# Attention in two resolutions and an ELU feed-forward: the order of all steps behind batch 0 written out as one list

## The chip, the cores and the metric

The kernel runs on one core of a Trainium2 chip. The metric is the device time of the program in microseconds. A core has five instruction queues that run beside each other, each in its own order: PE (TensorE, matrix products), DVE (VectorE), ACT (ScalarE), POOL (GpSimd) and SP (SyncE, which here only issues DMAs). ACT and POOL can issue DMAs too. Matrix products go to PSUM, which has few banks, so a bank must be read out before PE can write it again.

## What is computed

Eight batches of eight heads, 576 positions of 64 numbers. Each head has a local attention (only keys less than 4 positions away) and an attention over sequences shortened by the mean of each four positions; the two results are added. The sum, as 4608 tokens of 512 numbers, goes through two dense layers with an ELU between them.

```python
q_d = q.reshape(B, H, Sd, factor, D).mean(axis=3)        # same for k and v; factor = 4
out_up = np.repeat(sm_attn(q_d, k_d, v_d), factor, axis=2)
mask = np.abs(pos[:, None] - pos[None, :]) < factor
scores = np.where(mask, scale * np.matmul(q, k.transpose(0, 1, 3, 2)), -1000000000.0)
attn_out = out_up + softmax(scores) @ v
x = np.ascontiguousarray(attn_out.transpose(0, 2, 1, 3)).reshape(B * S, H * D)
h = x @ w_in                                             # 512 -> 2048
g = np.where(h > 0.0, h, alpha * (np.exp(np.minimum(h, 0.0)) - 1.0))
out = g @ w_out                                          # 2048 -> 512
```

## The kernel before

Attention works on pairs of heads, four pairs j to a batch b. For a pair the steps are: load q, k and v (SP, L165 and L178) into one of 11 fp32 stage buffers; cast them to fp16 on POOL (L201, L204, L211), which frees the stage; turn q and k on PE by products with an identity (L223, L232), which also sums fours; copy the turned tiles to SBUF (ACT, with sums on DVE); sum v in fours on PE (L285); scores (L311, L321); exp on ACT (L333, L339); mask on DVE (L348). After the four pairs come the denominators (PE L374) and their reciprocal (DVE L380). The reciprocals are spread over partitions: in batches 0 and 1 by matmuls with SEL (L410), later through DRAM, with a store of rd (L385) and a load of rcb (L395) on ACT's queue. Then the output products (L438, L444), two multiplications on DVE (L455, L458) and one or two additions on POOL (L465) that write x.

The dense layers work on nine tiles t of 512 tokens. mm1 has 16 steps of four 512-column matmuls (L498); behind each stand an exp on ACT (L503), a min-and-add (L504) and a max-and-add (L507) on DVE. mm2 has 16 steps of four matmuls (L518); each fourth ends a block of 128 tokens, which ACT copies to os (L524) and SP stores (L526). A batch is 576 tokens and a tile 512, so tile t needs parts of one or two batches: tile 0 only batch 0, tile 1 the last 64 tokens of batch 0 and 448 of batch 1.

Nothing moves an instruction after it is recorded (`manual_schedule`, L529): each engine runs its instructions in the order in which the Python code makes them. Batch 0 is made by `first_batch`. After it, functions that each record the steps of several engines (`mm1`, `mm2`, `scores`, `transposes`, `outputs`, `second_loads` and others) are given a time by `at(time, fn, ...)`, and the events are recorded sorted by that time. A function's steps thus enter all queues together: `mm2` records matmuls, copy and store in one go, `mm1` matmuls, exp and both elu steps.

The weights are loaded by `wload` on POOL's queue (L146): four parts of WI in batch 0, between the third and the fourth cast of v, and four parts of WO at the end of batch 0. Batch 1's first load waits through a 1x1 copy on POOL (L158) that reads element `gts[0][0:1, 7, 0:1]`, so it starts when the eighth elu of tile 0 is done.

Of the kernel before, what the change touches and what calls it, by code (L numbers as in the profile page):

```python
# [71 lines left out]
def kernel(  # L72
# [188 lines left out]
    def copy_k(b, j, tk, copy, copy_sums):  # L261
        _, kt, kd = stT[(b, j)]
        t4 = tk[:, :, 0:GW].rearrange("p g (c w) -> p g c w", w=QW)
        copy(
            out=kt[:, PAD : PAD + S].rearrange("p (g c u) -> p g c u", g=2, c=3),
            in_=t4[:, :, :, 0:QB],
        )
        copy_sums(
            out=kd[:].rearrange("p (g c n) -> p g c n", g=2, c=3), in_=t4[:, :, :, QB:QW]
        )  # L270

# [23 lines left out]

    def transposes(b, j):
        tq, tk = two("tq"), two("tk")
        new_qk(b, j)
        turned(b, j, "q", tq)
        vsum_mm(b, j, tq[:, :, GW : GW + 128])  # L300
        turned(b, j, "k", tk)
        copy_q(b, j, tq, nc.scalar.copy)
        vsum_copy(b, j, tq[:, :, GW : GW + 128])
        copy_k(b, j, tk, nc.scalar.copy, nc.vector.tensor_copy)
# [45 lines left out]
    def scores(b, j):  # L350
        sc = [two("sc"), two("sc")]
        sc_local(b, j, sc)
        sc_down(b, j, sc)
        for e in range(2):
            exp_local(b, j, sc, e)
            exp_down(b, j, sc, e)
        masked(b, j)
        stT.pop((b, j))


    def denominators(b, den):
# [118 lines left out]
    def outputs(b, j0):  # L480
        rcb = stR[b]
        lgs = {}
        for j in (j0, j0 + 1):
            lgs[j] = two("lg")
            out_mm(b, j, lgs[j])
        for j in (j0, j0 + 1):
            out_x(b, j, lgs[j], rcb)
# [4 lines left out]
    def mm1(t, fc):
        if fc == 0:
            gts[t] = sb.tile([128, FCN, TBLK], FP16, tag="gt", bufs=2, name="gt")
        hp = bank("misc" if t == 0 and fc % 2 else "hp", "hp")
        x = xts[t]
        for dc in range(DMC):
            nc.tensor.matmul(  # L498
                hp[:], WI[:, dc, 128 * fc : 128 * fc + 128], x[:, dc, :],
                start=(dc == 0), stop=(dc == DMC - 1),  # L500
            )
        e = sb.tile([128, TBLK], FP16, tag="e", bufs=3, name="e")
        nc.scalar.activation(out=e[:], in_=hp[:], func=AF.Exp)  # L503
        nc.vector.tensor_scalar(  # L504
            out=e[:], in0=e[:], scalar1=1.0, scalar2=-1.0, op0=AB.min, op1=AB.add
        )
        nc.vector.scalar_tensor_tensor(  # L507
            out=gts[t][:, fc, :], in0=hp[:], scalar=0.0, op0=AB.max, in1=e[:], op1=AB.add
        )

    def mm2(t, i):

        tt, part = i // 4, i % 4
        if part == 0:
            ops[t] = bank("misc", "op")
        op_ = ops[t]
        for fc in range(4 * part, 4 * part + 4):
            nc.tensor.matmul(  # L518
                op_[:], gts[t][:, fc, 128 * tt : 128 * tt + 128], WO[:, fc, :],
                start=(fc == 0), stop=(fc == FCN - 1),  # L520
            )
# [218 lines left out]
```

## Time and profile before

| | us |
|---|---|
| median of 3 runs | 403.9 |
| lowest and highest run | 394.77 and 430.42 |
| the profiled execution | 396.93 |
| its span, first to last instruction | 395.1 |

| engine | busy us | share of the span |
|---|---|---|
| PE, matmuls | 355.3 | 90% |
| DVE | 244.8 | 62% |
| ACT | 204.2 | 52% |
| POOL | 127.1 | 32% |

The page cuts the span into 40 slices of some 9.9 us; a digit is the busy share of a slice in tenths, and PEclk is the clock granted to PE:

```profile
PE   2778988948876898899999999999999999999996
DVE  2845964433875665796579748966885675555510
POOL 2548062065541582183218322831240040000000
PEclk9999999686997899999999999999999999999999
DMA  8989993069999997977784958543000500100112
```

A share over the whole span is a mean of stages with different limits, so a stage is read from its own slices. A busy PE is not always PE at its full pace: the pace follows from how many matmuls a stretch holds. A row of the timeline has the start, the duration, the engine, the line and the operation, and in brackets how long the engine stood idle before and what ended that.

### The profile page before, as it was taken

The numbers are of one execution on the slowest core, as the hardware profiler recorded it, in microseconds if no ns is written. First come the engines' busy times: TensorE is split into PE (matmuls) and PEld (weight loads), VectorE is DVE, ScalarE is ACT, GpSimd is POOL, SyncE is SP. The second block draws the span as 40 slices with busy tenths as digits, with TensorE's granted clock in tenths as the row PEclk, the third lists the DMA queues.
The fourth block names the chain that finished last, engine by engine and source line by source line (L and its number), as shares of the span: only waits on it lengthen the run. The fifth ranks groups of instructions, "written<-read, shape, count | busy, mean of one in ns | idle before, by whom it ended". The sixth has DMA issues, their size and how long they took to land.

```text
span 395.1 us, 9269 instructions
## 1 busy us (share of the span) xinstructions
PE 355.3 (90%) x3792; PEld 189.8 (48%) x3792; DVE 244.8 (62%) x468; ACT 204.2 (52%) x389; POOL 127.1 (32%) x181
## 2 busy tenths in 40 slices
PE   2778988948876898899999999999999999999996
PEld 2664444624443455455545555555554444444442
DVE  2845964433875665796579748966885675555510
ACT  3533657234865375657566655667474434444321
POOL 2548062065541582183218322831240040000000
PEclk9999999686997899999999999999999999999999
DMA  8989993069999997977784958543000500100112
GB/s 262 170 131 144 238 276 105 2 126 200 200 183 154 163 201 136 190 151 153 138 192 94 181 127 177 115 96 103 29 28 30 128 28 28 53 27 36 46 53 80
DMA packets 116260, 49.17 MB, mean 124 GB/s; under 512 B 102154, under 2 KB 109434, under 8 KB 116218
## 3 DMA queue, kind: packets, MB, share of 16 engines
q1 hardware_dynamic: 107082, 39.33, 49.5%
q0 software_dynamic: 4224, 4.19, 6.7%
q10 hardware_dynamic: 4912, 5.07, 5.9%
q8 instruction: 29, 0.48, 0.6%
q14 instruction: 13, 0.11, 0.1%
HBM read 43.23 MB, written 9.55 MB: 134 GB/s over the span
## 4 chain that ended last, share of the span: by engine, by line
PE 70%; DMA 14%; ACT 5%; DVE 5%; POOL 2%; issue 2%; ACTq 1%; SPq 0%; POOLq 0%; DVEq 0%
PE op L518 30%; PE hp L498 26%; DMA v<-in_v_dram 4%; DMA rd<-rc 4%; PE lg L438 2%; PE sc L311 2%; ACT pex L333 2%; DMA rcb<-rd 2%; PE tq L285 2%; DVE gt L507 2%; PE den L374 2%; DMA SEL<-SELc 2%; PE tq L223 2%; PE tk L223 1%; DMA q<-in_q_dram 1%
## 5 line engine op out<-in xcount | busy, mean ns | idle before, releaser
L498 PE MATMUL hp<-xt,WI 128*128 128x512 f16 x576 | 150.9, 390 | 2.8 <-DVE gt L507 1.7
L518 PE MATMUL op<-WO,gt 128*128 128x512 f16 x576 | 145.7, 382 | 0.0
L503 ACT ACTIVATE e<-hp 128x512 f16<-128x512 f32 x144 | 86.5, 602 | 102.1 <-PE hp L498 88.9
L507 DVE SCALAR_TENSOR_TENSOR gt<-hp,e 128x512 f16<-128x512 f32 x144 | 99.6, 692 | 5.4
L504 DVE TENSOR_SCALAR e<-e 128x512 f16<-128x512 f16 x144 | 55.4, 384 | 56.8 <-ACT e L503 54.6
L498 PEld LDWEIGHTS <-WI 128*128 128x128 f16 x576 | 54.9, 100 | 67.1 <-issue 10.4
L518 PEld LDWEIGHTS <-gt 128*128 128x128 f16 x576 | 54.2, 98 | 64.1 <-issue 1.3
L465 POOL TENSOR_TENSOR xt<-ln,gn 128x64 f16<-128x64 f16 (+7 forms) x64 | 42.1, 688 | 122.2 <-DVE ln L458 122.2
L333 ACT ACTIVATE pex<-sc 112x576 f16<-112x576 f32 x64 | 41.0, 647 | 14.5 <-PE sc L321 10.3
L348 DVE TENSOR_TENSOR mex<-pex,MASK 112x1152 f16<-112x1152 f16 x32 | 27.0, 843 | 25.6 <-ACT pex L333 25.3
L259 ACT CAST qt<-tq 128x720 f16<-128x720 f32 x24 | 18.3, 763 | 29.9 <-PE tq L285 27.6
L211 POOL CAST v<-v 112x768 f16<-112x768 f32 x32 | 28.7, 898 | 12.1 <-DMA v<-in_v_dram 12.1
L204 POOL CAST q<-q 96x768 f16<-96x768 f32 x24 | 20.8, 868 | 33.2 <-issue 21.2
L524 ACT COPY os<-op 128x512 f32<-128x512 f32 x36 | 21.2, 588 | 17.9 <-PE op L518 17.5
L339 ACT ACTIVATE dex<-sc 72x288 f16<-72x288 f32 x64 | 25.5, 404 | 2.8 <-PE sc L321 2.8
L458 DVE TENSOR_TENSOR ln<-lg,rcb 128x576 f16<-128x576 f32 x32 | 24.0, 749 | 0.0
L311 PEld LDWEIGHTS <-kt 64*112 64x112 f16 x384 | 14.5, 140 | 18.1 <-issue 5.5
L311 PE MATMUL sc<-qt,kt 64*112 64x96 f16 x384 | 18.9, 231 | 4.5 <-ACT dex L339 1.4
L204 POOL CAST k<-k 96x768 f16<-96x768 f32 x24 | 20.3, 847 | 4.4 <-DMA k<-in_k_dram 4.4
L293 DVE CAST vd<-tq 72x256 f16<-72x256 f32 x24 | 9.9, 414 | 18.2 <-ACT qt L259 18.1
L223 PE MATMUL tq<-I,q 96*128 96x120 f16 x144 | 12.1, 222 | 8.8 <-POOL q L204 5.0
L285 PEld LDWEIGHTS <-VR 112*72 112x72 f16 x192 | 15.2, 132 | 5.7 <-issue 3.9
(49 smaller groups left out, 244.3 us busy)
## 6 DMA issues: line engine op xcount, KB each, us to landing
v<-in_v_dram SPq DMA_DIRECT2D x30, 336.0 KB, 6.4
q<-in_q_dram SPq DMA_DIRECT2D x32, 288.0 KB, 5.3
k<-in_k_dram SPq DMA_DIRECT2D x32, 288.0 KB, 5.9
out_dram<-os SPq DMA_DIRECT2D x36, 256.0 KB, 2.3
rcb<-rd ACTq DMA_DIRECT2D x12, 360.0 KB, 5.5
WI<-in_moe_w_in_dram POOLq DMA_DIRECT2D x4, 512.0 KB, 8.6
WO<-in_moe_w_out_dram POOLq DMA_DIRECT2D x4, 512.0 KB, 9.2
v<-in_v_dram SPq DMA_DIRECT2D x2, 308.0 KB, 6.3
```

The lines of the kernel that those rows point to most:

```text
L204: nc.gpsimd.tensor_copy(out=t, in_=x.rearrange("p (e c d) -> p c e d", e=2, d=D))
L211: nc.gpsimd.tensor_copy(out=t[:], in_=st32.pop(("v", b, j)).rearrange("p (e c) d -> p c e d", e=2))
L311: nc.tensor.matmul(sc[e][0:KW, c // 3, QB * (c % 3) : QB * (c % 3) + QB], kt[r, QB * c : QB * c + KW], q_of(b, j, r, c), start=True, stop= ...
L333: nc.scalar.activation(out=stS[(b, j)][2][:, e, :].rearrange("p (g u) -> p g u", g=2), in_=sc[e][0:KW, :, 0:HB], func=AF.Exp, scale=SCALE,)
L339: nc.scalar.activation(out=stS[(b, j)][1][:, e], in_=sc[e][0:KG, :, HB : HB + SD], func=AF.Exp, scale=SCALE / 16.0,)
L348: nc.vector.tensor_tensor(out=mex[:], in0=pex[:], in1=mk2, op=AB.mult)
L465: nc.gpsimd.tensor_tensor(out=xt(t)[:, j, t0 - TBLK * t : t1 - TBLK * t], in0=ln[:, a:z], in1=_rep4(gn[:, a // 4 : z // 4]), op=AB.add,)
L498: nc.tensor.matmul(hp[:], WI[:, dc, 128 * fc : 128 * fc + 128], x[:, dc, :], start=(dc == 0), stop=(dc == DMC - 1),)
L503: nc.scalar.activation(out=e[:], in_=hp[:], func=AF.Exp)
L504: nc.vector.tensor_scalar(out=e[:], in0=e[:], scalar1=1.0, scalar2=-1.0, op0=AB.min, op1=AB.add)
L507: nc.vector.scalar_tensor_tensor(out=gts[t][:, fc, :], in0=hp[:], scalar=0.0, op0=AB.max, in1=e[:], op1=AB.add)
L518: nc.tensor.matmul(op_[:], gts[t][:, fc, 128 * tt : 128 * tt + 128], WO[:, fc, :], start=(fc == 0), stop=(fc == FCN - 1),)
```

## The change

The functions that record several engines' steps together and the list of timed events are gone. Behind batch 0 a text of 1398 words, ORDER, is read from left to right, and each word records one step of one engine: L load, C cast, T turn, A copy away, F sums of fours, SC scores, E0 and E1 exps, M mask, VS and VD sums of v and their copy, KD sums of k, DEN, RC, RB, RBC and SO, SI denominators, reciprocals and their spreading, OUT, MUL and X outputs, mm1, e, m, g and mm2 dense layers, oc and st copy and store of an output block. The steps themselves are the same; their place in each queue is new. Apart from the list:

- stores of output blocks go out on ACT's queue instead of SP's;
- batch 1's first load waits for the last x of tile 0, not for its eighth elu;
- in batch 0 all four casts of v stand ahead of the loads of WI on POOL;
- in batch 0 PE gets extra matmuls on a constant tile, written to PSUM tiles that are then overwritten: 9 of 512 columns ahead of the first turn, 8 of 128 columns ahead of each further turn, and 3 of 512 ahead of the first scores.

```diff
+ORDER = """
+mm1.0.0 mm1.0.1 e.0.0 mm1.0.2 m.0.0 e.0.1 g.0.0 mm1.0.3 m.0.1 e.0.2 g.0.1 mm1.0.4 m.0.2 e.0.3
+g.0.2 Lq1.0 X0.0.1 mm1.0.5 X0.1.1 Lk1.0 e.0.4 m.0.3 Lq1.1 g.0.3 X0.2.1 mm1.0.6 X0.3.1 Lk1.1
...
+    BUSY = sb.tile([128, 512], FP16, tag="busy", bufs=1, name="busy")
+    nc.vector.memset(BUSY[:], 0.5)
+    def keep_busy(tile_, n, w):
+        for _ in range(n):
+            nc.tensor.matmul(
+                tile_[:, 0, 0:w], BUSY[:, 0:128], BUSY[:, 0:w], start=True, stop=True
+            )
...
     def early_turn(b, j, copy_k):
         tq, tk = two("tq"), two("tk")
+        if b == 0:
+            keep_busy(tq, *((9, 512) if j == 0 else (8, 128)))
...
             if j + 2 == NPAIR - 1:
-                for i in range(3):
+                for i in range(NPAIR):
                     cast_v(0, i)
                 for i in range(4):
                     wload(i)
-                cast_v(0, 3)
             sc = [more("sc"), more("sc")]
+            if j == 0:
+                keep_busy(sc[0], 3, 512)
...
-    def second_loads():
-        load_qk(1, 0, gts[0][0:1, 7, 0:1])
...
+        if (n, b, j) == ("q", 1, 0):
+            nc.gpsimd.tensor_copy(out=t[0:1, 0:1], in_=xts[0][0:1, NPAIR - 1, 0:1])
...
-            nc.sync.dma_start(out=out[r : r + 128, :], in_=os_[:])
+        nc.scalar.dma_start(out=out[r : r + 128, :], in_=oss.pop((t, tt))[:])
...
-    for _, _, fn, args in sorted(events, key=lambda e: e[:2]):
-        fn(*args)
+    for word in ORDER.split():
...
+        does[name](*(int(i) for i in rest.split(".") if i))
```

How the list moves instructions is shown at three places, as the built programs have them.

SP's queue from batch 1's loads of v on. Before:

```order
L178 DMA v_810<-in_v_dram 112x12x64
L178 DMA v_812<-in_v_dram 112x12x64
L178 DMA v_814<-in_v_dram 112x12x64
L526 DMA out_dram<-os 128x512 x4
L165 DMA q_1561<-in_q_dram 96x12x64
L165 DMA k_1563<-in_k_dram 96x12x64
L178 DMA v_1565<-in_v_dram 112x12x64
```

The same place now:

```order
L292 DMA v_860<-in_v_dram 112x12x64
L292 DMA v_863<-in_v_dram 112x12x64
L292 DMA v_894<-in_v_dram 112x12x64
L681 DMA q_899<-in_q_dram 96x12x64
L681 DMA k_935<-in_k_dram 96x12x64
L292 DMA v_959<-in_v_dram 112x12x64
```

The four stores of tile 0 stood between the loads of batches 1 and 2; now the loads follow each other, and SP holds no store at all.

POOL's queue from batch 0's casts of v to the first load of batch 1 (the 1x1 cast lets that load start). Before:

```order
L211 CAST v_251<-v_110 112x768
L146 DMA WI<-in_moe_w_in_dram 128x4x512 x4
L211 CAST v_257<-v_112 112x768
L465 ISA
L465 TENSOR_TENSOR xt<-ln,gn 128x512 x4
L146 DMA WO<-in_moe_w_out_dram 128x4x512 x4
L465 TENSOR_TENSOR xt<-ln,gn 128x64 x4
L158 CAST q_791<-gt 1x1
```

The same place now:

```order
L325 CAST v_273<-v_112 112x768
L325 CAST v_275<-v_114 112x768
L260 DMA WI<-in_moe_w_in_dram 128x4x512 x4
L556 ISA
L556 TENSOR_TENSOR xt<-ln,gn 128x512 x4
L260 DMA WO<-in_moe_w_out_dram 128x4x512 x4
L673 CAST q_791<-xt 1x1
L556 TENSOR_TENSOR xt<-ln,gn 128x64 x4
```

The fourth cast of v changed places with WI, and the 1x1 cast, which now reads x, stands ahead of the additions for tile 1. Further on, before, all eight additions of batch 1 stood ahead of batch 2's first cast; now ten of those twelve casts stand ahead of the first addition and the other two between additions.

ACT's queue around the spreading of batch 2's reciprocals (rd is the store to DRAM, rcb the load back). Before:

```order
L385 DMA rd<-rc 128x72
L259 CAST qt<-tq 128x720
L264 CAST kt_75<-tk 128x576
L503 ACTIVATE e<-hp 128x512
L395 DMA rcb<-rd 64x4x720 x2
```

The same place now:

```order
L476 DMA rd<-rc 128x72
L426 ACTIVATE pex<-sc 112x576
L432 ACTIVATE dex<-sc 72x288
L426 ACTIVATE pex<-sc 112x576
L432 ACTIVATE dex<-sc 72x288
L829 ACTIVATE e<-hp 128x512 x2
L720 CAST kt_80<-tk 128x576
L486 DMA rcb<-rd 64x4x720 x2
```

Three steps stood between the store and the load that needs it; now there are seven.

## Rows read from the trace of the kernel before

**Rows 1.** Table of stretches: us, each engine's busy us (instructions), clock, DMA share, GB/s

```profile
34.10:92.00 57.90, 46.92 (x576) 25.44 (x576) 29.96 (x57) 27.48 (x57) 21.39 (x33) 0.89 0.74 148
92.00:188.60 96.60, 84.54 (x1045) 46.51 (x1044) 66.59 (x129) 59.75 (x115) 42.62 (x55) 0.94 1.04 173
188.60:392.00 203.40, 202.15 (x1740) 100.93 (x1740) 130.72 (x254) 102.90 (x189) 46.59 (x63) 1.00 0.36 85
...
322.00:377.00 55.00, 55.00 (x256) 24.91 (x255) 31.61 (x64) 23.54 (x41) 0.35 (x1) 1.00 0.10 39
...
62.80:83.00 20.20, 17.51 (x319) 10.81 (x317) 8.86 (x17) 8.57 (x22) 2.95 (x4) 0.83 0.06 22
...
86.20:96.40 10.20, 6.42 (x42) 3.69 (x42) 1.87 (x5) 2.49 (x4) 6.01 (x10) 0.50 1.36 199
...
130.00:188.60 58.60, 54.30 (x697) 29.95 (x696) 41.25 (x80) 34.91 (x67) 27.82 (x37) 1.00 0.97 167
```

**Rows 2.** The same table for mm1's matmuls (L498) alone: PE, PEld, clock, DMA

```profile
187.69:301.22 113.53, 49.39 (x193) 17.47 (x192) 1.00 0.54 114
```

**Rows 3.** The same for mm2's matmuls (L518) alone

```profile
187.69:301.22 113.53, 49.40 (x192) 17.80 (x192) 1.00 0.54 114
```

**Rows 4.** Timeline of PE, in batch 0 and in the output steps of batch 1

```profile
15.26 1.01 PE L311 MATMUL sc<-qt,kt 64*112 64x96 f16 x12 [0.43 <-ACT dex L339]
...
76.16 0.45 PE L438 MATMUL lg<-mex,v 112*64 112x96 f16 x12
...
76.67 0.49 PE L410 MATMUL rb<-rc,SEL 32*128 32x72 f16 x10
77.09 1.04 PE L518 MATMUL op<-WO,gt 128*128 128x512 f16 x4
```

**Rows 5.** Timeline of SP's queue (issue start and duration, waits between merged issues included)

```profile
57.76 25.19 SPq L526 DMA_DIRECT2D out_dram<-os  x4
83.04 0.38 SPq L165 DMA_DIRECT2D q<-in_q_dram  x1
...
89.79 1.74 SPq L165 DMA_DIRECT2D q<-in_q_dram  x1
...
94.48 1.75 SPq L165 DMA_DIRECT2D q<-in_q_dram  x1
```

**Rows 6.** The chain that ended last, in order of time, 0 to 50 us

```profile
10.39 9.96 DMA v<-in_v_dram
...
21.23 3.08 POOL WI L146 x4
...
25.20 0.80 PE vs L285 x6
...
30.57 0.26 PE lg L444 x4
...
34.11 5.07 PE hp L498 x13
```

**Rows 7.** Timeline of DVE at the end of tile 0's elus

```profile
47.57 0.69 DVE L507 SCALAR_TENSOR_TENSOR gt<-hp,e 128x512 f16<-128x512 f32 x1
...
48.49 0.69 DVE L507 SCALAR_TENSOR_TENSOR gt<-hp,e 128x512 f16<-128x512 f32 x1
...
52.26 0.74 DVE L253 TENSOR_REDUCE qt<-qt 128x144 f16<-128x576 f16 x1
```

**Rows 8.** The page's groups: busy us, mean ns of one, idle before

```profile
L348 DVE TENSOR_TENSOR mex<-pex,MASK 112x1152 f16<-112x1152 f16 x32 | 27.0, 843 | 25.6 <-ACT pex L333 25.3
...
L293 DVE CAST vd<-tq 72x256 f16<-72x256 f32 x24 | 9.9, 414 | 18.2 <-ACT qt L259 18.1
```

**Rows 9.** Timeline of ACT behind the load of rcb

```profile
123.45 0.60 ACT L503 ACTIVATE e<-hp 128x512 f16<-128x512 f32 x1 [3.79 <-issue]
```

**Rows 10.** DMA issues of two lines: ns shortest, median, longest; first and last start

```profile
L526 SPq DMA_DIRECT2D out_dram<-os x36: 332/333/3122, 57.8 to 392.1; - x36
...
L385 ACTq DMA_DIRECT2D rd<-rc x6: 326/329/345, 117.3 to 303.5; - x6
```

More of the change, by code (lines that the diff above doesn't have):

```diff
@@ L259, in copy_q @@
         copy(out=stT[(b, j)][0][:], in_=tq[:, :, 0:GW])
[L261 to L270, printed above, removed]
     def q_of(b, j, r, c):
@@ L294, in vsum_copy @@
         stV[(b, j)][1] = vd
[L296 to L304, printed above, removed]
     def sc_local(b, j, sc):
@@ L348, in masked, with den_mm @@
         nc.vector.tensor_tensor(out=mex[:], in0=pex[:], in1=mk2, op=AB.mult)
[L350 to L361, printed above, removed]
+    def den_mm(b, den):
         for e in range(2):
@@ L478, in out_x @@
             t0 = t1
[L480 to L487, printed above, removed]
-    gts, ops = {}, {}
[L492 to L521, printed above, removed]
-        if part == 3:
-            os_ = sb.tile([128, DM], FP32, tag="os", bufs=2, name="os")
-            nc.scalar.copy(out=os_[:], in_=op_[:])
-            r = TBLK * t + 128 * tt
-            nc.sync.dma_start(out=out[r : r + 128, :], in_=os_[:])
+    gts, ops = {}, {}
     ctx.enter_context(tc.manual_schedule())
@@ new lines, in turn, with away @@
+    def turn(n, b, j):
+        x = tp[(n, b, j)] = two("t" + n)
+        turned(b, j, n, x)
+        if n == "q" and not nines(b):
+            vsum_mm(b, j, x[:, :, GW : GW + 128])
+    def away(n, b, j):
+        x, had = tp[(n, b, j)], stT.get((b, j), ())
+        if n == "q":
+            qt = sb.tile([128, 2 * GW], FP16, tag="qt", bufs=3, name="qt")
+            parts = (qt,)
+        else:
+            kt, kd = KT[nkt[0] % 3], sb.tile([128, SD], FP16, tag="kd", bufs=3, name="kd")
+            nkt[0] += 1
+            parts = (kt, kd)
+        stT[(b, j)] = parts + had if n == "q" else had + parts
+        if nines(b):
+            copy_nines(qt[:, 0:S] if n == "q" else kt[:, PAD : PAD + S], x, nc.scalar.copy)
+        elif n == "q":
+            nc.scalar.copy(out=qt[:], in_=x[:, :, 0:GW])
+        else:
+            t4 = x[:, :, 0:GW].rearrange("p g (c w) -> p g c w", w=QW)
+            nc.scalar.copy(
+                out=kt[:, PAD : PAD + S].rearrange("p (g c u) -> p g c u", g=2, c=3),
+                in_=t4[:, :, :, 0:QB],
+            )
@@ new lines, with x_one, mm1_one @@
+    lns = {}
+    def x_one(b, j, t):
+        if b == 0:
+            fn, *args = later0[j]
+            fn(*args)
+            return
+        ln, gn = lns[(b, j)]
+        t0, t1 = max(TBLK * t, S * b), min(TBLK * (t + 1), S * (b + 1))
+        a, z = t0 - S * b, t1 - S * b
+        nc.gpsimd.tensor_tensor(
+            out=xt(t)[:, j, t0 - TBLK * t : t1 - TBLK * t], in0=ln[:, a:z],
+            in1=_rep4(gn[:, a // 4 : z // 4]), op=AB.add,
+        )
+    def mm1_one(t, fc):
+        if fc == 0:
+            gts[t] = sb.tile([128, FCN, TBLK], FP16, tag="gt", bufs=2, name="gt")
+        hp = hps[(t, fc)] = bank("misc" if t == 0 and fc % 2 else "hp", "hp")
+        x = xts[t]
+        for dc in range(DMC):
+            nc.tensor.matmul(
+                hp[:], WI[:, dc, 128 * fc : 128 * fc + 128], x[:, dc, :],
+                start=(dc == 0), stop=(dc == DMC - 1),
+            )
@@ new lines, in mm2_one, with out_copy @@
+    def mm2_one(t, i):
+        tt, part = i // 4, i % 4
+        if part == 0:
+            ops[(t, tt)] = bank("misc", "op")
+        for fc in range(4 * part, 4 * part + 4):
+            nc.tensor.matmul(
+                ops[(t, tt)][:], gts[t][:, fc, 128 * tt : 128 * tt + 128], WO[:, fc, :],
+                start=(fc == 0), stop=(fc == FCN - 1),
+            )
+    def out_copy(t, tt):
+        oss[(t, tt)] = sb.tile([128, DM], FP32, tag="os", bufs=2, name="os")
+        nc.scalar.copy(out=oss[(t, tt)][:], in_=ops[(t, tt)][:])
```

310 lines of the change are left out of this document (230 added, 80 removed).

## The prediction

> **What bounds the kernel now.** I read the table of stretches first, since the share of the whole span (PE 90%) mixes stages. Three stretches stand out [rows 1]. From 188.6 us to the end PE is busy 202.15 of 203.4 us. From 34.1 to 92 it is busy 46.92 of 57.9 us at a mean granted clock of 0.89, and from 92 to 188.6 it is busy 84.54 of 96.6 us at 0.94. So the last half is PE's own work, and only the first half can give time back. The next reading must say how much.
>
> Price of PE's work. A group here is one mm1 or mm2 step of four 512-column matmuls. In 322 to 377 us nothing else runs, and 256 matmuls (64 groups) take 55.0 us [rows 1]: 0.859 us a group. Three batches of attention lie between the first denominator matmul at 187.69 us and the fourth at 301.22 us, 113.53 us in all; 193 and 192 matmuls of the two lines run there [rows 2, 3], 96.25 groups or 82.7 us. The rest, 30.8 us, is three batches of attention: 10.3 us each, small waits included. Batch 1 also spreads its reciprocals by matmul, 0.42 us a pair (from 76.67 to 77.09) [rows 4], so it costs 10.3 + 4 x 0.42 = 12.0 us.
>
> Now the account of each stretch, counting steps in the order of before.
> - A, 34.1 to 92 us: 31.5 groups (27.1), batch 1 (12.0) and the first turn of batch 2 (about 1.0, well under half of a pair's 10.3 / 4). That is 40.1 us of work in 57.9: 17.8 lost.
> - B, 92 to 188.6 us: 59.25 groups (50.9) and batches 2 to 4 without that turn (1.0) and without batch 4's four output steps (0.5 each, from 76.16 to 76.67 [rows 4]): 27.9. That is 78.8 us of work in 96.6: 17.8 lost.
> - C, 188.6 us to the end: 197 groups (169.2), 30.9 and 2.0: 202.1 in 203.4. Nothing to win.
>
> Why A loses. SP's queue has the answer. Four output stores of token tile 0 stand ahead of all of batch 2's loads; the last waits for an os that is made at 82 us, and the first q of batch 2 is issued at 83.04 [rows 5]. From 62.8 to 83 us the DMA moved 22 GB/s [rows 1]. When the data comes, PE has lost its clock: 0.50 granted from 86.2 to 96.4 us, with PE busy only 6.42 of 10.2 [rows 1]. SP then issues one pair's q, k and v every 4.7 us (89.79 to 94.48 [rows 5]), and B begins by running at the pace of these landings.
>
> **The change, part by part.**
>
> Front, batch 0. The chain of waits to the first mm1 goes through the landing of v, the issue of four weight loads on POOL (3.08 us), and only then the last cast of v; mm1 flows from 34.11 us [rows 6]. The new order casts first. That cast would start where the issue now starts, after DMA traffic has nearly stopped, so the V sums, now at 25.20 us, come earlier. Nothing to 3.08 us can come of it; I take half, 1.6 us, because the V sums still have the denominators ahead of them on PE. The weights are issued one cast later, and their landing has room: the first group needs only the first quarter.
>
> The filler matmuls are in no row of before. Their lower bound is a loss: 24 of 128 columns at the slow pace (13 matmuls of 512 in 5.07 us [rows 6], so 0.39 each and 0.1 for 128 columns) are 2.4 us, 0.8 a pair, against an idle time of 0.43 us per pair ahead of the scores [rows 4]. About 0.4 a pair is not covered; over three pairs 1.2 us comes off the 1.6. Of the other 12 fillers nine run while the first inputs land and three while the first k is copied out. The upper bound is that the clock is up from the start. Then the seven PE pieces of the chain from 25.20 to 30.83 us, 4.05 us in all, halve (2.0), and the 13 matmuls of 5.07 us take 2.8 at the full pace (2.3) [rows 6]. So the front gives between 0.4 and 5.9 us. I take 1.6, near the lower end, because the clock stayed down through a batch 0 in which the page's slices have PE busy 7 to 9 tenths.
>
> The Trainium skill's page "TensorE: Matmul & The Clock Gate" (Part 1) says that the slow clock is the state of rest and that activity releases it. By that the fillers would earn the upper bound and the sum below would be 363.1 us; the slow 13 matmuls at 34.11 us agree that batch 0 leaves the clock down.
>
> A. The 36 stores move to ACT, and SP's queue is loads alone. Batch 1's first load waits for the last x of tile 0, not for the eighth elu: its POOL copy follows directly on the 4 issues of WO (taken as 3.08, as for WI): 34.1 - 1.6 + 3.1 gives about 35.6 us. Before it was near 44 us, four elu pairs ahead of the twelfth add at 47.57 [rows 7]. Its turns, sums and scores then go in between mm1.0.9 and mm2.0.4 rather than behind mm1.0.15. DVE now becomes the limit there. Up to the last elu of tile 0 its list holds 16 elu pairs at 0.92 us (from 47.57 to 48.49), 8 reductions of 0.74 [rows 7], 4 copies of 0.41 and 2 masks of 0.84 [rows 8]: 14.7 + 5.9 + 1.7 + 1.7 = 24.0 us. PE's part up to there is 17 groups and half of batch 1, 20.6 us, and hides under it. What remains to the same point (first turn of batch 2 done) is PE's: 40.1 - 20.6 = 19.5. The stretch becomes 24.0 + 19.5 = 43.5 us against 57.9: **14.4 us gained**. Bounds: no better than 17.8, and, if half of the waits come back elsewhere, 7.5.
>
> The Trainium skill's page "DMA: Bandwidth & Descriptors" (Issuing engines are not separate DMA queues) speaks against the move of the stores: all queues share the same DMA engines, and another issuing engine saves only issue time. By that alone 36 stores of 0.33 us would be worth at most 12 us of SP and nothing on the path, and without the gain in A the sum would be 381.8 us. I do not follow it here, because what SP loses in these rows is a wait, not issue time or bandwidth.
>
> B. With the loads some 30 us earlier, turns no longer wait for landings. The second cause in B is ACT: its queue holds the load of rcb three short steps (two copies, one elu exp) behind the store of rd, and ACT stands 3.79 us until rd has landed [rows 9]; soon after, the clock falls again. In the new list four exps, two elu exps and a copy lie between the two. POOL, too, no longer puts batch 1's eight adds ahead of the casts of batch 2. What stays is the normal waiting between engines, which I price by the rest of B: 130 to 188.6 us has PE idle 4.3 us at full clock [rows 1]. I keep 4.3 of 17.8: **13.5 us gained**, with bounds 17.8 and 8.9 (half).
>
> ACT pays for the stores. Each costs its queue 0.33 us, the price of the rd store that ACT issues now [rows 10]; 36 make 12 us. ACT is busy 59.75 of 96.6 us in B and 102.9 of 203.4 in C [rows 1], so its idle time hides them. Without that cover, at PE's pace, it would be 12 us.
>
> **Sum.** Against the profiled execution's own 396.9 us: 396.9 - 1.6 - 14.4 - 13.5 = 367.4 us. That execution is 1.7% under the median shown, 403.9, and within its runs (394.77 to 430.42); the change takes stalls away, so I give the same figure for an undisturbed run.
>
> **The rivals.**
> 1. Half of it. A listed order holds every engine to one sequence, so one late landing holds back PE at the head of its queue. The place I fear is mm1.0.10: Tq1.0 stands before it, and batch 1's q and k now share the DMA with WO. For it: the DMA moved 148 GB/s over stretch A and 199 GB/s at its best in these rows [rows 1], so the same bytes need 57.9 x 148 / 199 = 43 us, hardly less than my 43.5. Against it: the loads of batch 2's later pairs are among those bytes. With the lower ends of all terms (0.4, 7.5, 8.9) the time is 380.1 us.
> 2. Nothing moves. The stores leave SP, but landings still set the pace: a batch of q, k and v needs 4 x 4.7 = 18.8 us of issue, and B's waits remain whole. If the earlier start only lets loads wait for free buffers (11 stages, each freed by a cast), the front and a third of A remain: 396.9 - 1.6 - 5.9 = 389.4 us, within 2%. Against it: the old order had the buffers free and the queue blocked.
> 3. Slower. The stores on ACT: on SP one issue took up to 3.12 us [rows 10] while the DMA rings were full, and ACT's next exp would wait behind each. Fifteen stores stand ahead of the last load in the list. ACT has 37 us of slack in B [rows 1], so nothing shows at 1 us each; at 3.12 us they take 47 us. The gain of 29.5 is gone when each puts 2 us on PE's path; at 2.6 us each the kernel would take 367.4 + 39 = 406 us. Against it: ACT's own DMAs in the same traffic took 0.33 us [rows 10].
>
> **How the numbers follow.** My forecast, 355 to 374 us: 0.66. Rival 1, 374 to 389: 0.19. Rival 2, within 2% (389 to 405): 0.08. Rival 3, above 405: 0.05. Better than 355: 0.02. Two per cent is about what a measurement of this kernel can tell from no change. So faster 0.87, same 0.08, slower 0.05. The low end is every upper bound at once: 396.9 - 5.9 - 17.8 - 17.8 = 355.4. The high end is rival 1 with 2 us for the stores: 382.
>
> **What would show it.** SP issues batch 2's first q before 55 us; the stores appear on ACT's queue near 0.33 us each; no stretch after 45 us with a granted clock of 0.50; mm1 of tile 1 starts near 76 us instead of 92; and the tail, from the first mm1 of tile 7 on, is as long as before. I am wrong if PE waits for q or k of batch 1 between 40 and 50 us (rival 1), if POOL waits for landings through batches 2 and 3 (rival 2), or if ACT's store issues exceed 1 us (rival 3).

## The result, and the profile after

The changed kernel takes **382.3 us** (median of 4 executions, 378.71 to 382.72) against 400.4 us for the kernel before beside it (394.77 to 430.42); the ratio is 0.964, with a 95% interval of 0.953 to 0.975. The ratio leaves out two executions of the kernel before (403.9 and 430.42 us) that ran in a slower state. The changed kernel is faster, as forecast, but by half of what was forecast: 367.4 us was given, with a range of 355.4 to 382.0. The profiled execution takes 382.56 us (span 380.8) against 396.93 before, so 14.4 us were won where 29.5 were forecast. (In the runs further down the kernel before takes 395.3 to 396.5 us, and the changed kernel's gain is read against that.)

The page of the kernel after, the span in 40 slices of some 9.5 us:

```profile
PE   8769849999987999899979999999999999999996
...
PEclk9987966999995999999998999999999999999999
DMA  7989999999989999495495952240012201011012
```

The table of stretches of the kernel after; columns as in [rows 1]: stretch, its length, busy us of PE, PEld (PE's weight loads), DVE, ACT and POOL, granted clock, DMA share (the time that packets took, over that of 16 DMA engines; it can pass 1), GB/s.

```profile
18.00:22.00 4.00, 3.31 (x157) 2.82 (x156) 2.40 (x5) 0.82 (x3) 3.48 (x5) 1.00 0.11 20
...
28.00:38.00 10.00, 9.98 (x35) 4.02 (x35) 6.87 (x15) 4.95 (x9) 4.18 (x10) 0.75 1.18 218
38.00:47.00 9.00, 7.52 (x129) 3.62 (x127) 6.49 (x12) 6.10 (x11) 4.04 (x7) 1.00 1.14 290
47.00:54.20 7.20, 1.70 (x21) 1.00 (x21) 3.42 (x6) 3.08 (x7) 2.13 (x3) 0.72 1.22 210
54.20:64.00 9.80, 9.41 (x86) 5.62 (x86) 5.49 (x11) 3.56 (x7) 4.14 (x5) 0.51 1.28 181
64.00:86.00 22.00, 21.81 (x366) 13.49 (x364) 10.07 (x21) 14.03 (x33) 14.16 (x16) 1.00 1.23 198
86.00:108.00 22.00, 21.11 (x275) 11.50 (x274) 17.93 (x35) 18.31 (x36) 9.30 (x13) 1.00 1.22 188
108.00:114.00 6.00, 4.88 (x44) 2.55 (x40) 4.76 (x10) 3.29 (x7) 2.42 (x3) 1.00 0.70 135
114.00:126.00 12.00, 10.07 (x105) 5.25 (x102) 4.98 (x11) 2.87 (x6) 5.13 (x7) 0.57 1.13 192
...
150.00:160.00 10.00, 8.70 (x109) 4.92 (x108) 7.87 (x17) 3.78 (x7) 7.30 (x11) 1.00 0.67 135
...
188.00:198.00 10.00, 8.82 (x85) 4.20 (x82) 4.62 (x10) 4.50 (x9) 2.97 (x4) 1.00 0.88 173
198.00:205.00 7.00, 6.12 (x62) 3.86 (x63) 3.98 (x9) 1.60 (x3) 5.77 (x9) 0.76 0.45 74
205.00:377.00 172.00, 172.00 (x1458) 84.80 (x1456) 103.90 (x213) 86.69 (x156) 32.35 (x46) 1.00 0.27 69
...
28.00:86.00 58.00, 50.42 (x631) 27.75 (x631) 32.34 (x63) 31.71 (x65) 28.65 (x39) 0.84 1.21 215
```

How the table becomes an account: in each stretch PE loses its idle time, and of its busy time the share that the granted clock is short (at 0.51 nearly half of 9.41 us). From 28 to 86 us, where the first mm1 of tile 1 starts, that is 7.6 us idle and 2.5 + 0.5 + 4.6 us by the clock, 15 us in all. From 86 to 205 us it is 7.4 us idle and 4.3 + 1.5 us by the clock, 13 us. Behind 205 us PE is never idle.

| | lost before | forecast | lost after |
|---|---|---|---|
| A, first mm1 of tile 0 to first mm1 of tile 1 | 17.8 | 3.4 | 15 |
| behind A (B and C) | 17.8 + 1.3 | 5.6 | 13 |
| start of mm1's flow | 34.1 us | 32.5 us | 28.0 us |

So the front gave 6.1 us (1.6 forecast), A gave 3 of 14.4, and what lies behind it 6 of 13.5: 15 us by this account, for the 14.4 measured. The first column prices the work, the last adds idle time and missing clock; added in this second way the kernel before lost 18.4 us in A (11.0 idle, 5.2 by the clock and 2.3 in the 13 slow matmuls at its start [rows 6]) and 18.4 behind it, which makes the gains 3 and 5 us. All of it holds for these two executions; e8 and e2 below show how far the front moves between executions.

The rows of the timelines behind this, PE first, then SP's queue, POOL, ACT's queue, DVE and once more PE; in brackets the idle time before and what ended it:

```profile
28.02 10.63 PE L822 MATMUL hp<-xt,WI 128*128 128x512 f16 x37 [0.43 <-POOL xt L556]
...
54.11 0.80 PE L388 MATMUL vs<-v,VR 112*72 112x128 f16 x6 [4.32 <-POOL v L325]
...
86.00 1.89 PE L822 MATMUL hp<-xt,WI 128*128 128x512 f16 x8
...
115.52 0.69 PE L529 MATMUL lg<-mex,v 112*64 112x96 f16 x12 [1.09 <-ACT dex L432]
...
37.81 15.72 SPq L292 DMA_DIRECT2D v<-in_v_dram  x4
53.62 1.86 SPq L681 DMA_DIRECT2D q<-in_q_dram  x1
...
53.23 0.83 POOL L325 CAST v<-v 112x768 f16<-112x768 f32 x1 [4.14 <-DMA v<-in_v_dram]
...
104.58 0.33 ACTq L476 DMA_DIRECT2D rd<-rc  x1
109.12 1.32 ACTq L486 DMA_DIRECT2D rcb<-rd  x2
...
118.95 0.31 DVE L792 TENSOR_TENSOR gn<-lg,rcb 128x144 f16<-128x144 f32 x1 [3.39 <-PE lg L529]
...
197.85 0.31 DVE L792 TENSOR_TENSOR gn<-lg,rcb 128x144 f16<-128x144 f32 x1 [4.11 <-DMA rcb<-rd]
...
198.88 0.45 PE L529 MATMUL lg<-mex,v 112*64 112x96 f16 x12 [2.06 <-DVE ln L795]
```

Three things stand out. First, SP's queue does what was forecast: batch 2's first q is issued at 53.62 us, where 25.19 us of waiting stood before [rows 5]. Yet tile 1 starts only at 86.00 us: its distance from the start of mm1 is 58.0 us, as long as before (57.9 us [rows 1]). Some 3 us of that are more work: the list has three of batch 2's four pairs turned ahead of tile 1, where before it was one, so PE's work in the stretch is 43 us (58.0 less the 15 lost), against 40.1. The DMA has no rest any more: its share is 1.1 to 1.3 in every stretch from 28 to 108 us, where before it fell to 0.06 [rows 1], and the 58 us move 58.0 x 215 = 12.5 MB instead of 57.9 x 148 = 8.6 MB. Second, PE stands 4.32 us at the V sums of batch 1's first pair, whose v lands late, and runs at a mean clock of 0.51 after it, near the lower of its two levels (1.2 of 2.4 GHz). From 64 us on PE is busy 21.81 of 22.00 us at full clock, so the 15 us are lost ahead of that, half as waits and half by the clock. Third, from the store of batch 2's reciprocals (104.58) to their first use (118.95) 14.4 us pass, and in batch 4 DVE and then PE stand for them (4.11 and 2.06 us). The row at 118.95 names PE's lg, but e4, which waits for no reciprocals, has the same product at 116.12.

### The profile page after: what moved, and what is told of

The parts are those of the page before. It is cut to its first block, busy times and chain, and to the rows that moved or that the text cites. A ratio compares the mean times of both kernels' runs of the same rounds, so it can differ in the third digit from the quotient of the medians.

```text
span 380.8 us, 9313 instructions
## 1 busy us (share of the span) xinstructions
PE 354.9 (93%) x3828; PEld 186.5 (49%) x3828; DVE 236.2 (62%) x469; ACT 206.9 (54%) x389; POOL 127.7 (34%) x181
## 4 chain that ended last, share of the span: by engine, by line
PE 72%; DMA 15%; ACT 3%; DVE 3%; POOL 2%; issue 1%; ACTq 1%; SPq 1%; DVEq 0%
PE op L848 31%; PE hp L822 26%; DMA v<-in_v_dram 6%; DMA rcb<-rd 4%; DMA q<-in_q_dram 3%; PE lg L529 3%; PE sc L404 2%; PE tq L337 2%; PE tq L388 2%; PE den L456 2%; PE tk L337 2%; DMA rd<-rc 1%; DMA VR<-VRc 1%; POOL xt L556 1%; PE lg L535 1%
## 5 line engine op out<-in xcount | busy, mean ns | idle before, releaser
L822 PE MATMUL hp<-xt,WI 128*128 128x512 f16 x576 | 143.5, 386 | 4.4 <-DVE gt L838 2.8
L848 PE MATMUL op<-WO,gt 128*128 128x512 f16 x576 | 143.8, 388 | 0.0
L829 ACT ACTIVATE e<-hp 128x512 f16<-128x512 f32 x144 | 85.7, 598 | 78.7 <-PE hp L822 72.1
L833 DVE TENSOR_SCALAR e<-e 128x512 f16<-128x512 f16 x144 | 52.2, 363 | 54.0 <-ACT e L829 53.1
L811 POOL TENSOR_TENSOR xt<-ln,gn 128x448 f16<-128x448 f16 (+7 forms) x56 | 37.7, 699 | 48.1 <-DVE ln L795 46.0
L441 DVE TENSOR_TENSOR mex<-pex,MASK 112x1152 f16<-112x1152 f16 x32 | 24.5, 765 | 11.9 <-ACT pex L426 11.7
L795 DVE TENSOR_TENSOR ln<-lg,rcb 128x576 f16<-128x576 f32 x28 | 20.9, 748 | 0.0
L792 DVE TENSOR_TENSOR gn<-lg,rcb 128x144 f16<-128x144 f32 x28 | 8.5, 302 | 19.7 <-PE lg L535 9.6
L529 PE MATMUL lg<-mex,v 112*64 112x96 f16 x384 | 15.1, 220 | 5.9 <-DVE ln L795 4.2
L404 PEld LDWEIGHTS <-kt 64*112 64x112 f16 x384 | 13.1, 129 | 15.3 <-issue 11.5
L529 PEld LDWEIGHTS <-v 112*64 112x64 f16 x384 | 11.4, 117 | 15.1 <-issue 6.8
## 6 DMA issues: line engine op xcount, KB each, us to landing
WO<-in_moe_w_out_dram POOLq DMA_DIRECT2D x4, 512.0 KB, 17.1
```

What stands on the lines that cost most here:

```text
L404: nc.tensor.matmul(sc[e][0:KW, c // 3, QB * (c % 3) : QB * (c % 3) + QB], kt[r, QB * c : QB * c + KW], q_of(b, j, r, c), start=True, stop= ...
L529: nc.tensor.matmul(l2[64 * e : 64 * e + 64, c // 3, QB * (c % 3) : QB * (c % 3) + QB], v16[:, c, e, :], mex[:, e, QB * c : QB * c + QB], s ...
L811: nc.gpsimd.tensor_tensor(out=xt(t)[:, j, t0 - TBLK * t : t1 - TBLK * t], in0=ln[:, a:z], in1=_rep4(gn[:, a // 4 : z // 4]), op=AB.add,)
L822: nc.tensor.matmul(hp[:], WI[:, dc, 128 * fc : 128 * fc + 128], x[:, dc, :], start=(dc == 0), stop=(dc == DMC - 1),)
L829: nc.scalar.activation(out=e[:], in_=hps[(t, fc)][:], func=AF.Exp)
L833: nc.vector.tensor_scalar(out=e[:], in0=e[:], scalar1=1.0, scalar2=-1.0, op0=AB.min, op1=AB.add)
```

## The experiments

Two theories follow. **D**: in stretch A the transfers set the pace, whatever the list and the start of mm1. **R**: behind A the way of the reciprocals through DRAM holds DVE, with it the PSUM banks that DVE has still to read, and so PE. Their rivals are the forecast's own reasons: the stores on SP (A and S), the fillers (F), and waits that merely follow from the order of the list.

| run | median us | lowest, highest | ratio to before (95%) | first elu exp of tile 1 |
|---|---|---|---|---|
| after | 382.3 | 378.7, 382.7 | 0.964 (0.953, 0.975) | 87.07 |
| e1 no fillers | 382.2 | 381.3, 384.3 | 0.967 (0.962, 0.973) | 87.79 |
| e2 stores on SP | 382.1 | 380.5, 382.9 | 0.965 (0.959, 0.971) | 89.15 |
| e3 WO late | 385.5 | 382.4, 387.3 | 0.974 (0.967, 0.981) | 88.49 |
| e4 no wait for reciprocals | 373.8 | 372.5, 375.5 | 0.945 (0.940, 0.951) | 87.61 |
| e5 a quarter of WO | 375.3 | 369.0, 377.4 | none | none |
| e6 e4 and e5 | 367.1 | 365.0, 369.6 | 0.926 (0.917, 0.934) | 81.55 |
| e7 outputs later in the list | 380.3 | 377.7, 385.1 | 0.957 (0.947, 0.968) | 87.37 |
| e8 before, stores on ACT | 402.5 | 399.6, 407.2 | 1.013 (1.010, 1.017) | 90.77 |
| e9 no gate | 381.4 | 375.6, 385.1 | none | 82.18 |
| e10 reciprocals on SP | 377.1 | 376.4, 379.6 | 0.957 (0.949, 0.964) | 85.90 |
| e11 e7 and e9 | 375.6 | 374.6, 378.7 | 0.952 (0.945, 0.959) | 81.35 |
| e12 e9 and e10 | **372.1** | 370.9, 375.5 | 0.938 (0.934, 0.943) | 81.43 |

One execution each of e5 and e6 took 1933 us; it is left out here (three others stay), and for e5 it was the profiled one, so that its trace is not used. "None" under the ratio means that none is on record. The last column is the start of the seventeenth of ACT's exps e<-hp (L829 in the kernel after), right behind the first mm1 step of tile 1: the end of stretch A.

**e1: no fillers.**

```diff
-        if b == 0:
-            keep_busy(tq, *((9, 512) if j == 0 else (8, 128)))
...
-            if j == 0:
-                keep_busy(sc[0], 3, 512)
```

> The changed kernel without its 36 filler matmuls ahead of and in batch 0; all else as changed. Theory F (the fillers raise the clock, and that is what made the front win 6.1 us): batch 0 runs at the slow pace again, the first full run of mm1 starts near 32 us instead of 28.0 and the kernel takes 386 to 389 us. Rival (the earlier cast of v made the front win, the fillers cost as much as they give): mm1 starts at 28 to 29 us and the time stays within 1.5 us of 382.

382.2 us: the fillers are worth nothing that these executions could show, and theory F falls. They do raise the clock early, which shows in the timeline of PE of the kernel after:

```profile
1.47 4.02 PE L234 MATMUL tq<-busy 128*128 128x512 f16 x9 [1.47 <-DVE busy L229]
...
6.24 0.82 PE L234 MATMUL sc<-busy 128*128 128x512 f16 x3
```

Nine fillers of 512 columns take 4.02 us, 0.45 each; the three behind them 0.82, 0.27 each. But the clock does not stay up: in the kernel after it is 0.75 on the mean from 28 to 38 us. Without fillers the first elu exp of tile 0 stands at 29.7 us, with them between 28.7 and 32.1 in the executions of after, e2 to e4, e7 and e10. In e1 the clock rises without them, though later: two equal runs of denominator matmuls take 0.72 us at 19.78 and 0.52 us at 20.51. So the front's gain is not theirs. Nor is it shown to be the earlier cast's, the other edit there, which was not tried alone. The front of the kernel before, unchanged in e8, has its flow of mm1 at 31.23 us there and at 34.11 in the trace of before; the changed front has it between 28.02 (after) and 31.38 (e2). Part of the 6.1 us can thus be the difference between two executions of the same front. And 3.4 us at the front move the end of stretch A by little (last column), which already speaks for D.

**e2 and e8: the stores.** e2 puts the changed kernel's stores back on SP; e8 moves the stores of the kernel before to ACT and leaves the rest.

```diff
 e2, the kernel after:
-        nc.scalar.dma_start(out=out[r : r + 128, :], in_=oss.pop((t, tt))[:])
+        nc.sync.dma_start(out=out[r : r + 128, :], in_=oss.pop((t, tt))[:])
 e8, the kernel before:
-            nc.sync.dma_start(out=out[r : r + 128, :], in_=os_[:])
+            nc.scalar.dma_start(out=out[r : r + 128, :], in_=os_[:])
```

> The changed kernel with its 36 output stores issued by SP again, each at the same place of the listed order. Theory S (the stores held SP's loads, so their move to ACT is part of the gain): the loads of batches 2 to 4 are issued later, as each store waits for its os at the head of SP's queue; 388 to 395 us. Rival (the list already puts each store right behind its copy, so SP waits little; the move is worth nothing): 380 to 384 us. Rival 3 of the prediction (the stores hurt on ACT): under 380 us.

> The kernel before with one edit: its 36 output stores are issued by ACT. Order and front are as before. Theory A of the prediction (the four stores at the head of SP's queue hold batch 2's loads for 25 us, and this is what costs stretch A): batch 2's first q is issued before 65 us instead of 83, and the time falls by 8 to 14 us, to 382 to 388 us. Rival (the store is only a symptom: the loads then run into the DMA that is busy with batch 1, or ACT issues the stores too late in its own order): 392 to 397 us, as before.

e2: 382.1 us, nothing, as its rival said. e8: 402.5 us, 1.3% slower than before: no gain either, but outside the 392 to 397 us of its rival, and for another reason than the two it names. e8's rows (of an execution of 406.3 us), SP's queue, POOL and PE:

```profile
54.34 1.85 SPq L165 DMA_DIRECT2D q<-in_q_dram  x1
...
77.12 0.95 POOL L465 TENSOR_TENSOR xt<-ln,gn 128x448 f16<-128x448 f16 x1 [15.31 <-DVE ln L458]
...
86.09 0.78 PE L223 MATMUL tq<-I,q 96*128 96x120 f16 x6 [5.07 <-POOL q L204]
...
31.23 14.50 PE L498 MATMUL hp<-xt,WI 128*128 128x512 f16 x61 [0.44 <-POOL xt L465]
```

The same waits in the kernel before:

```profile
78.95 0.95 POOL L465 TENSOR_TENSOR xt<-ln,gn 128x448 f16<-128x448 f16 x1 [15.37 <-DVE ln L458]
...
87.86 0.78 PE L223 MATMUL tq<-I,q 96*128 96x120 f16 x6 [5.01 <-POOL q L204]
```

SP issues batch 2's first q 29 us earlier (54.34 against 83.04 [rows 5]), and PE waits for its cast as long as before. POOL stands 15.31 us at batch 1's adds, which its order holds ahead of the casts of batch 2. It stood there 15.37 us in the kernel before too, so the trace of before already showed this second holder. The wait had two holders, one behind the other; taking away SP's leaves the other. Where e8's further 6 us come from wasn't followed up.

**e3: WO late.** WO's four loads are issued behind the casts of k of pairs 2 and 3 and of v of pairs 0 and 1.

```diff
-        for i in range(4, 8):
-            wload(i)
...
-Fk1.0 Cq1.2 mm1.0.12 Aq1.1 g.0.9 Ck1.2 Lq2.1 Ak1.1 ...
+Fk1.0 Cq1.2 mm1.0.12 Aq1.1 g.0.9 Ck1.2 WO0 Lq2.1 Ak1.1 ...
```

> The changed kernel with the four loads of WO issued later, one each behind the casts of batch 1's k of pairs 2 and 3 and of its v of pairs 0 and 1, so that batch 1's loads have the DMA alone. Theory L (WO and batch 1 share the DMA, v lands late, PE stands at the V sums of pair 0 and then runs at half clock): the V sums of pair 0 start before 47 us instead of 54.1, PE idles under 3 us instead of 7.4 between 38 and 64 us, no half clock there, 371 to 376 us. Rival (the DMA is the limit whatever the order; PE waits for WO at mm2.0.0 or for batch 2 instead): 380 to 384 us.

385.5 us (382.4 to 387.3), no gain, and above its rival's 380 to 384. The V sums of the first pair start at 46.76 us without a wait for v, and the last elu exp of tile 0 at 49.7 instead of 58.6 us. It buys nothing: PE then waits 4.42 us for the v of pair 3 and 2.69 us for a v of batch 2, and tile 1 starts at 88.49. The wait at the V sums of the first pair was only one place where late transfers showed.

**e4, e5 and e6: the two suspects taken away.** e4 lets the products of batches 2 to 7 read batch 1's reciprocals (kept in a buffer of their own); e5 loads a quarter of WO; e6 does both.

```diff
 e4:
-        lg, rcb = lgs[(b, j)], rcbs[b]
+        lg, rcb = lgs[(b, j)], rcbs[1]
 e5:
-        for i in range(4, 8):
-            wload(i)
+        wload(4)
...
-WO[:, fc, :]
+WO[:, fc % 4, :]
```

> The changed kernel in which the products of batches 2 to 7 read batch 1's spread reciprocals, so that they wait for no reciprocals of their own; these are still stored to rd and loaded to rcb as before, with nobody waiting. It leaves out dividing batches 2 to 7 by their own sums. Theory R (the way of the reciprocals through DRAM holds DVE, PSUM banks and so PE in batches 2 and 4): the waits of 0.84 us at 119 and 2.06 us at 197 us go, with the half clock after the second; 376 to 379 us. If the half clock from 115 us hangs on it too: 372 to 376 us. Rival (these waits are covered by others): 381 to 384 us.

> The changed kernel with only the first of the four loads of WO; every mm2 step multiplies by that quarter. It leaves out three quarters of the second weight, so that some 9 us of DMA time are taken away from the stretch in which batch 1 and 2 are loaded. Theory D (from 28 us to the first mm1 of tile 1 the transfers set the pace, whatever the list or the start of mm1): the V sums of pair 0 start near 48 us instead of 54, the first elu exp of tile 1 stands near 80 us instead of 87, and the time is 375 to 378 us. Rival (the engines' own order sets that stretch; the wait for v turns into others): the exp at 85 to 87 us, 380 to 383 us.

> Both at once: only the first quarter of WO is loaded, and batches 2 to 7 multiply by batch 1's reciprocals without waiting for their own. It leaves out the same two parts as those runs. If the two causes (theories D and R) are separate and make up what the forecast missed, the savings add up: 373.8 less 5 to 7 us, 366 to 369 us, which is the time that was forecast. If one hides the other, 371 to 374 us.

e4 gives 373.8 us, 8.5 less than after. Its table of stretches at the places that lost in the kernel after, its first product of batch 2 on DVE, and a row of PE in e6:

```profile
108.00:126.00 18.00, 16.07 (x185) 9.01 (x183) 12.23 (x27) 10.16 (x19) 11.98 (x16) 1.00 0.98 180
150.00:160.00 10.00, 9.94 (x95) 5.85 (x93) 8.17 (x17) 7.71 (x14) 7.46 (x10) 1.00 1.12 188
188.00:198.00 10.00, 10.00 (x129) 5.97 (x128) 5.76 (x13) 4.45 (x8) 9.23 (x14) 1.00 0.83 191
198.00:205.00 7.00, 7.00 (x61) 3.73 (x59) 5.90 (x11) 5.21 (x10) 3.83 (x5) 1.00 1.33 196
...
116.12 0.31 DVE L792 TENSOR_TENSOR gn<-lg,rcb 128x144 f16<-128x144 f32 x1 [0.64 <-PE lg L535]
...
110.11 0.69 PE L529 MATMUL lg<-mex,v 112*64 112x96 f16 x12 [1.09 <-ACT dex L432]
```

The granted clock is 1.00 in all of e4's stretches, and from 150 us to the tail PE is next to never idle. From 86 to 205 us PE idles 2.5 us in e4 and 7.4 in after. So of the 10.1 us between these two executions 4.8 are waits, and the clock has most of the rest. How much of the clock hangs on the reciprocals is not shown. In the kernel after the half pace of batch 2's stretch is there at 115.52 (0.69 us for a run that takes 0.45 at full pace), ahead of PE's first wait for their products at 119.98; and e6, which waits for no reciprocals either, has it at the same step. That half clock is worth 4.3 us in the kernel after.

e5 gives 375.3 us (middle of three, which lie between 369.0 and 377.4). e6 gives 367.1 us, 15 less than after: the savings add up. That the sum is the time that was forecast is chance, since e6 leaves out loads that the kernel needs. In e6 the end of stretch A is 81.55 us, though its mm1 starts 3 us later than in the kernel after (31.8 against 28.7 us).

**e7: output steps later in the list.** Two to four mm2 steps move ahead of the outputs of batches 2 and 4 and one ahead of those of batch 3, here at batch 2:

```diff
-... OUT2.0 mm2.1.3 MUL2.0 Cv3.3 OUT2.1 oc.1.0 M3.1 Lk4.3 OUT2.2 ...
+... mm2.1.4 mm2.1.5 mm2.1.3 oc.1.0 M3.1 st.1.0 mm2.1.6 OUT2.0 MUL2.0 Cv3.3 OUT2.1 Lk4.3
+mm2.1.7 oc.1.1 st.1.1 OUT2.2 ...
```

> The changed kernel, complete, with a changed list: two to four mm2 steps of the tile before are put ahead of the output steps of batches 2 and 4 and one ahead of those of batch 3, taken from places behind them, so that PE has work while the reciprocals come back. Theory R: most of what the run without the wait for the reciprocals gave comes back without leaving anything out, 374 to 378 us, and no half clock from 115 us. Rival (the output steps are then late for the adds of the next tile, and PE waits there for x instead): 381 to 386 us.

380.3 us (377.7 to 385.1), not told apart from 382.3 and short of the 374 to 378 expected. The waits at the outputs mostly go (0.91 us is left at 196.53), the clock is full from 108 to 126 us, and a wait of 2.34 us for DVE's elu appears at 129.66, at the third step of tile 2. Filling a wait with steps of the same tile moved it.

**e9 and e11: the transfers earlier.** Batch 1's first q no longer waits for tile 0's last add; e11 adds e7's list.

```diff
-        if (n, b, j) == ("q", 1, 0):
-            nc.gpsimd.tensor_copy(out=t[0:1, 0:1], in_=xts[0][0:1, NPAIR - 1, 0:1])
```

> The changed kernel, complete, without the one copy on POOL that holds batch 1's first q behind the last add of tile 0, so that SP issues batch 1's loads as soon as batch 0's casts free their buffers, near 15 to 20 us instead of 31. Theory D (from 22 us to the first mm1 of tile 1 the transfers set the pace, and between 18 and 22 us the DMA stands idle): the idle 4 us are filled, batch 1's V sums come before 50 us, the first elu exp of tile 1 stands at 82 to 85 us instead of 87, 377 to 380 us, though mm1 itself starts later (30 to 33 us) as WI shares the DMA. Rival (WI comes so late that mm1's own start moves the stretch by as much): the exp at 87 us or later, 382 to 386 us.

> The changed kernel, complete, with both edits: batch 1's loads without their gate, and the list in which mm2 steps stand ahead of the output steps of batches 2 to 4. Theories D and R name separate stretches, so the two savings should add: about 2 us of the second and 2 to 5 us of the first, 374 to 378 us. If the stretches aren't separate (the time won before tile 1 only lets PE wait longer for the reciprocals): 378 to 381 us.

e9's row of the stretch in which the DMA stood idle (0.11 in the kernel after), and ACT's exp:

```profile
18.00:22.00 4.00, 3.36 (x150) 2.85 (x151) 2.62 (x6) 0.82 (x3) 3.17 (x5) 1.00 1.00 295
...
82.18 0.60 ACT L827 ACTIVATE e<-hp 128x512 f16<-128x512 f32 x1
```

The gap is filled, mm1 starts 3 us later (its first exp at 31.9), and stretch A still ends 4.9 us earlier, at 82.18, as theory D said. The total of e9 alone (381.4, 375.6 to 385.1) is not told apart from 382.3 and misses the 377 to 380 expected. In its trace the time is given back in batches 2 to 4: PE runs at 0.65 and 0.75 of the clock from 108 to 114 and 114 to 126 us, and waits 1.91 us at 150.22 and 2.44 at 196.88 behind the products that need the reciprocals. With e7's list it is 375.6 us.

**e10 and e12: the reciprocals on SP.** rd's store and rcb's loads move to SP, and loads of batches 4 to 6 are listed behind them, so that SP's own waiting keeps loads off the DMA. e12 does this without the gate, and with pair 1 of batch 4 behind them too (its list is shown).

```diff
-        nc.scalar.dma_start(out=rd[:], in_=stR[b][:])
+        nc.sync.dma_start(out=rd[:], in_=stR[b][:])
...
-Ak3.1 g.1.11 Ck3.3 SI2 KD3.1 Cq4.0 ...
+Ak3.1 g.1.11 Ck3.3 SI2 Lq4.1 Lk4.1 Lv4.1 Lq4.2 Lk4.2 Lv4.2 KD3.1 Cq4.0 ...
```

> The changed kernel, complete, with the store of rd and the loads of rcb issued by SP instead of ACT, and the loads of pairs 2 of batches 4 and 5 and of q of pair 3 of batch 6 listed behind them, so that SP's own waiting keeps further loads off the DMA while the reciprocals go out and come back. Theory R with traffic (the reciprocals take 14.5 us there and back because they share the DMA with loads): from the store of rd to the first product 8 to 10 us, the wait at 197 us gone, 375 to 379 us. Rival (SP reaches the store later than ACT did, since it stands in its own waits for buffers, and the loads held back are late): 382 to 390 us.

> The changed kernel, complete, with both of the findings: batch 1's loads without their gate, and the reciprocals' store and loads on SP, now with the loads of pairs 1 and 2 of batch 4 behind them, so that the store of batch 2's rd meets an emptier DMA. Theories D and R: the first elu exp of tile 1 stands near 82 us, the products of batches 2 to 4 wait less than 2 us each for their reciprocals, and the time is 369 to 373 us, below all complete kernels so far. Rival (the loads held back are late in batch 4, or the time won before tile 1 is given back at batch 2's reciprocals as without the move to SP): 375 to 380 us.

e10 gives 377.1 us, within its range, though its reciprocals take 11.6 us from store to first product in batches 2 and 3 and not 8 to 10; the wait at 197 us is gone. e12 gives **372.1 us**: the fastest complete kernel here, 10 us under the changed one and 24 under the one before. e12's rows, SP's queue in batches 2 and 4, then DVE, and its stretch A from the start of mm1:

```profile
100.68 1.92 SPq L476 DMA_DIRECT2D rd<-rc  x1
105.77 1.34 SPq L486 DMA_DIRECT2D rcb<-rd  x2
...
178.30 0.34 SPq L476 DMA_DIRECT2D rd<-rc  x1
181.10 1.25 SPq L486 DMA_DIRECT2D rcb<-rd  x2
...
112.22 0.31 DVE L790 TENSOR_TENSOR gn<-lg,rcb 128x144 f16<-128x144 f32 x1 [3.31 <-DMA rcb<-rd]
...
189.14 0.31 DVE L790 TENSOR_TENSOR gn<-lg,rcb 128x144 f16<-128x144 f32 x1 [1.86 <-PE lg L535]
...
31.02:80.36 49.34, 45.78 (x634) 25.64 (x635) 33.74 (x63) 31.25 (x65) 27.80 (x38) 0.97 1.24 193
```

From store to first product it is 11.5 us in batch 2 instead of 14.4, and in batch 4 DVE waits for PE's products and no longer for the reciprocals. Batches 2 and 3 (at 145.35) still wait 3.3 us on DVE, more than the 2 us expected, and the time is within what was expected. In stretch A 5 us are lost (3.6 idle, 1.4 by the clock) instead of 15: with the loads earlier, the waits go and with them the half clock.

## Why the prediction was half right

- **Where the time could be won** was right: behind 205 us PE is busy 172.00 of 172.00 us, and all that was won lies before.
- **Front, 1.6 us**: mis-sized for this execution. The flow of mm1 starts 6.1 us earlier, a little over the upper bound of 5.9. The reason given for the bound was wrong too: e1 shows that the fillers don't carry it, and since unchanged fronts differ by some 3 us from one execution to another (31.23 and 34.11; 28.02 and 31.38), nearness to the bound is in part luck. By the Trainium skill's page "TensorE: Matmul & The Clock Gate" (Part 1) the fillers would have earned the upper bound. They raised the clock as it says (0.45 us a matmul, then 0.27), but the total does not show it.
- **A, 14.4 us**: the step that failed. "Why A loses. SP's queue has the answer" named a wait that was real and went away, but e8 shows that its removal alone is worth nothing, and e2 that the list is fast with the stores on SP. POOL's order, the second holder, the forecast did name, but as a part of B and without a price. The stretch was then priced by DVE's and PE's work, 43.5 us, as if a load had landed once SP could issue it. It took 58.0 us, some 3 of them more work: up to tile 0's last elu exp 31 us passed where 24.0 were given, with PE waiting for v and then at half clock. Rival 1 weighed the DMA: "the same bytes need 57.9 x 148 / 199 = 43 us", hardly less than the 43.5, and it set against this that loads of batch 2 are among those bytes. The bytes grew instead: with SP free, loads of later batches enter the stretch, 12.5 MB instead of 8.6. The seven traces of changed kernels with all loads and the gate (after, e1 to e4, e7, e10) end A between 85.90 and 89.15 us, though they start mm1 3.4 us apart and one of them has the v of the first pair 7 us earlier; only fewer bytes (e6) or an earlier start of the transfers (e9, e11, e12) end it near 82. In the kernel after the transfers act through the waits ahead of 64 us and the 4.6 us of clock lost behind the longest of them; from there on PE's own work paces the stretch.
- **The place feared**, q and k of batch 1 ahead of mm1.0.10, was nearly right: PE waited up to 0.96 us there, and 4.32 us for v behind them. Of the forecast's rivals 1 (380.1 us) came closest, with luck in the split: it has 0.4, 7.5 and 8.9 us where the account above has 6.1, 3 and 5 to 6.
- **The stores on ACT** were free as said, 0.33 us each (0.334 to 0.472 us), but so they were on SP, and rival 3's 3.12 us, of an issue that stood at a DMA share of 1.33 in the kernel before, did not come up. The Trainium skill's page "DMA: Bandwidth & Descriptors" (Issuing engines are not separate DMA queues) spoke against the move and was right (e2: 382.1 us with the stores on SP, 382.3 on ACT). The 381.8 us worked out beside it is near the measured time by luck: that sum gives A nothing and B all of its 13.5.
- **B, 13.5 us**: the second step that failed; 5 to 6 us came. I moved the load of rcb away from the store of rd and called the rest "the normal waiting between engines", priced by 4.3 us. That put the reciprocals' way at nothing. It is about as long as it was, 14.4 us from the store of batch 2's rd to its first use, against 15.0 in the kernel before, where the product then hardly waits:

```profile
117.26 0.34 ACTq L385 DMA_DIRECT2D rd<-rc  x1
...
132.30 0.31 DVE L455 TENSOR_TENSOR gn<-lg,rcb 128x144 f16<-128x144 f32 x1 [0.34 <-DMA k<-in_k_dram]
```

  What is new is that the list has the outputs ready earlier than that. e4 gives the price of this, 8.5 us between the medians; 4.8 are waits, and how much of the clock belongs to it is not settled.
- **The signs**: batch 2's q before 55 us (53.62) and the stores' price came as told, and the end is PE's work alone as before; no half clock behind 45 us (0.51 from 54.2 to 64 us), and tile 1 at 76 us (86.00), did not. A sign can come true and prove only its own step.

Left open: why e8 is slower than before, what the front's edits are worth, why the clock falls in batch 2, and how much of A's end the WO loads alone would move, since e5 has no trace of an ordinary execution.

## What to carry over

A long wait at the head of one queue is worth only what remains when the next holder of the same data takes over: look for who else stands behind it (here POOL's order, then the DMA), and count the bytes that the freed queue will add. Where the DMA share stands above 1 from end to end of a stretch and PE waits for landings in it, price it by its transfers as well; here starting them earlier or loading less moved its end, and neither an earlier mm1 nor a later place for WO did. A small transfer on the path behind large loads needs a lead as long as its way under load (here 14 to 15 us) or loads held back while it runs. And an execution's stretch can differ from another's by more than a term of the forecast, so compare several before a term is called won.
